# First MLP's in-projection of two of six token blocks in 2x2 block products, seven in place of eight, with the weight units combined on GpSimd

## The chip, the cores and the metric

The kernel runs on one core of a Trainium2 chip. Its time is the device time of one execution in microseconds; below are the median and the limits of three runs. One more execution was profiled, and its trace is what the rows come from.

## The reference

Three parts follow each other. Retention attention over 4 batches, 8 heads, 768 steps, 64 wide; then an MLP on 3072 tokens of 512 with a hidden width of 2048; then a gated MLP with a hidden width of 1536.

```
state = gamma * state + k[:, :, t] (x) v[:, :, t]        # per head, 768 steps
y[:, :, t] = scale * q[:, :, t] @ state
x = y, as 3072 rows of 512
h = maximum(x @ w_in, 0);  x = (h * h) @ w_out           # 512 -> 2048 -> 512
xn = x / sqrt(mean(x * x) + 1e-6) * rms_g
out = (silu(xn @ w_gate) * (xn @ w_val)) @ w_out2        # 512 -> 1536 -> 512
```

The weights arrive as 64-bit floats and are turned into float32 on the chip.

## The kernel before

**Arithmetic.** Every product is made of float32r halves: a number is a high part (a cast on ScalarE) and a low part (a subtraction on VectorE, L97), and a product takes three matmuls, high by high, high by low and low by high (`mm3`, L243 to L246). "A step of 12 matmuls" is 4 pieces of the contraction times three.

**Tokens.** The 3072 tokens are six blocks of 512 (0 to 5). Blocks 0 and 1 pass the first MLP in `block1`, hidden piece f = 0 to 15 by piece: 12 matmuls in, relu and square (`act1`), a split into halves named s, 12 matmuls out. Blocks 2 and 3 pass `in_phase(xs)`, 16 hidden pieces f by two blocks t, so that (f, t) names a step, and then `out_1`. Blocks 4 and 5 do the same with `in_phase(xs2)` and `out_2`. Then the second MLP runs in three pairs of blocks.

**Seven products for eight.** `out_1`, `out_2` and the second MLP already work with 2x2 block products: operand sums, seven products P1 to P7, result sums. Their weight operands ("units", 128x2x512, made by `made_units`, L143) lie in DRAM (`uo`, `uo2`) and come one by one into a ring of seven tiles (`ring`, `next_unit`, `unit_done`, L374 to L384); the load of the unit that comes seven later is issued when the products of a unit are done. The in-projection of the first MLP works with plain pieces: in blocks 0 to 3 the weights w_i lie in SBUF, for blocks 4 and 5 they were stored to DRAM (`wi`) and come through the same ring.

**Attention.** It is spread over the first stages as visits: the state and outputs of one chunk of the sequence. A visit's output leaves PSUM banks pr as the operand xh, xl of a later block (`Operand.put`, L262: a copy on ScalarE, a low part on VectorE). A visit scales the state (st) and two operands (vkt, qnt) in advance, many of these on GpSimd (L737, L748, L825).

**Weights.** `tick` (L221) turns one raw weight of 128x512 into float32: `magnitude` on ScalarE (L203) reads the raw tile, two operations on VectorE (L208, L209) finish it, and then the raw load of three steps later is issued on SP (L197). 32 steps serve the first MLP and 36 the second. Ticks are placed by hand between products. ScalarE, VectorE, GpSimd and SP each work in program order, so what is written between two products also stands there in the queue of its engine.

**Order.** The program is written in one order by hand; `between` and `after` callbacks of a phase put work of other engines between the products. The second in-projection has these:

```
for f in range(NF1):
    w = w_of(f)
    for t in range(2):
        proj(w, xs[t], ph[t])
        between(f, t)
        ...
        after(f, t)
```

Of the kernel before, what the change touches and what calls it, by code (L numbers as in the profile page):

```python
# [42 lines left out]
W2_SOON = 20  # L43
OPEN_AT = 12
PREP_IN = 10
# [12 lines left out]
def retention_then_two_mlps(  # L58
# [13 lines left out]
    wi = [dram.tile([128, 2, 512], F32, name=f"wi{f}") for f in range(NF1)]  # L72
# [30 lines left out]
    def sub(out_, a, b):  # L103
        nc.vector.tensor_tensor(out=out_, in0=a, in1=b, op=ALU.subtract)  # L104

    def plus(out_, a, b):
        nc.vector.tensor_tensor(out=out_, in0=a, in1=b, op=ALU.add)  # L107
# [35 lines left out]
    def made_units(to, q, rows, spare):  # L143
        a11, a21 = (rows[0][:, :, h * HALF:(h + 1) * HALF] for h in range(2))
        a12, a22 = (rows[1][:, :, h * HALF:(h + 1) * HALF] for h in range(2))
# [8 lines left out]
        plus(sm, a21, a22)  # L154
        sub(a21, a11, a21)
# [3 lines left out]
        sub(sm, sm, a11)  # L159
        put(P7, a21)  # L160
        yield
        sub(a12, a12, sm)
# [85 lines left out]
    class Operand:  # L248
# [13 lines left out]
        def put(self, o, banks):  # L262
            n = KC // len(banks)
            for k, src in enumerate(banks):
                a = slice(n * k, n * k + n) if self.whole else slice(0, n)
                h, l = (t[0 if self.whole else k][:, a, o] for t in self.t)
                split(h, l, src, nc.vector)

# [226 lines left out]
    def prep_x(j, y, subs_first=False):  # L495
# [14 lines left out]
        def put(k, src):  # L510
            X[k] = [slot("xop", F32R) for _ in range(2)]
            split(*X[k], src, nc.vector)
# [120 lines left out]
    ORDER = (P2, P1, P5, P6, P7, P3, P4)  # L633

# [45 lines left out]

    with tc.manual_schedule():
# [24 lines left out]
        def load_v(c):  # L706
            nc.sync.dma_start(both[c], vk[c])
# [295 lines left out]

        def early0(f):
            tick(low_first=at[0] < 5, ahead=at[0] > 8)

        def late0(f):
            tick(low_first=at[0] < 5)

# [6 lines left out]
        def factory(q):  # L1016
            rows = [slot("rows") for _ in range(2)]
            for r in range(2):
                for c in range(2):
                    w = W[("o", 4 * q + 2 * r + c)].bitcast(F32)  # L1020
                    plus(rows[r][:, c, :], w[:, 0, :], w[:, 1, :])
                    yield
            yield from made_units(uo, q, rows, lambda: cf.tile([128, 512], F32, tag="f", name="sm"))

        def all_units():
            for q in range(NQ):
                yield from factory(q)

        def keep_out(f):
            keep_units(uo, f, W[("o", f)])  # L1030
            nc.sync.dma_start(wi[f], W[("i", f)].bitcast(F32))

        xs = []
        made = all_units()
# [12 lines left out]

        def last1(f):
            stores()
            if f >= 5:  # L1050
                for _ in range(3):
                    next(made, None)

        block1(1, cur, sink1, (0, 2, 4, 6, 8, 10, 12, 14), early1, keep_out, last1)
# [6 lines left out]
        def sink2(c):  # L1061
            t = c // B - 4
            if t == len(xs2):
                xs2.append(Operand(t == 0))
# [16 lines left out]
        stream += wi  # L1081
# [9 lines left out]
        def after1(f, t):  # L1091
# [11 lines left out]
            elif f % 2 == 0 and f < 8:  # L1103
                tick()
            if t or f not in (2, 4, 6, 8):
                make_some()
            if 2 * f + t >= 24 and len(ring) < 7:
# [9 lines left out]
        while at[0] < upto[0] or at[0] - 1 in done:  # L1117
            tick()
# [5 lines left out]
        while makers:  # L1124
            make_some()
        stores()
        out_1.hi(3)

        def extra1(n, y):
            if n == NOUT - 7:  # L1130
                more_steps(len(steps))
            if NOUT - 4 <= n < NOUT - 2:
                tick()

# [28 lines left out]
        def between2(f, t):  # L1163
            background()
            if (f, t) == (3, 0):
                sums(pa[0])
            if f == OPEN_AT and t == 0:
# [4 lines left out]
            if f >= 8 and next(prep_count) < PREP_IN:  # L1172
                next(prep[0], None)

        prep_count = iter(range(10 ** 6))

        def after2(f, t):
            if t == 1:
                unit_done()
            if f < OPEN_AT and (t == 0 or f in (2, 6)):  # L1180
                stores()
                tick()
            if t == 1 and 3 <= f < 7:
                if f == 3:
                    yn.extend(big(f"yn{t_}") for t_ in range(2))
                h, t_ = ((1, 0), (0, 0), (0, 1), (1, 1))[f - 3]
                nc.sync.dma_start(yn[t_][:, 2 * h:2 * h + 2, :], ys[t_][:, 2 * h:2 * h + 2, :])
            if f == 5 and t == 0:
                prep[0] = prep_x(0, {(h, t_): yn[t_][:, 2 * h:2 * h + 2, :] for h in range(2) for t_ in range(2)}, True)
                next(prep[0])  # L1190
            if (f, t) in ((13, 1), (14, 1)):
                out_2.hi(f - 13)
                out_2.lo(f - 13)
            if f == 15:
                if t:
                    out_2.lo(2)
                out_2.hi(2 + t)

        def w_of2(f):
            return next_unit()  # L1200

        in_phase(xs2, w_of2, after2, between2)
        next(prep[0], None)
# [9 lines left out]
        def extra2(n, y):  # L1213
            if n == 0:
# [192 lines left out]
```

## Time and profile before

| | us |
|---|---|
| median of 3 runs | 1104.43 |
| lowest, highest | 1103.22, 1105.47 |
| span of the profiled execution, first to last instruction | 1102.2 |
| TensorE busy in it | 1093.3 |
| VectorE, ScalarE, GpSimd busy | 732.5, 544.9, 64.3 |

The profiled execution has no time of its own beside its span; the median of the runs is 2.2 us above it. Stages by the trace, in us from the span's start: block 0 from 16 to 115, block 1 to 235, the in-projection of blocks 2 and 3 to 342, `out_1` to 419, the in-projection of blocks 4 and 5 to 506, `out_2` to 584, the second MLP to the end. TensorE's granted clock is 1.00 (2.4 GHz) in all of them.

### The profile page before, as it was taken

The page shows a single profiled execution, that of the slowest core. Times are in us where ns is not written, and L with a number is a line of the kernel's source. Part 1 is how long each engine was busy: PE and PEld are TensorE (multiplying, and loading weights), DVE is VectorE, ACT ScalarE, POOL GpSimd, SP SyncE. Part 2 cuts the span into 40 slices and gives each one's busy share as a digit, 9 for nine tenths or more (in the row PEclk, how much of TensorE's full clock was granted, in tenths as well). Part 3 has the DMA queues.
Part 4 walks back from the last instruction along what each step waited for, and adds up shares of the span by engine and source line. Part 5 has one row for each costly group of instructions (what it writes and reads, how often), then busy time and mean ns, then how long its engine had stood idle before and what let it go on. Part 6 is the DMA issues. An engine that isn't in the chain of part 4 may idle for free.

```text
span 1102.2 us, 16497 instructions
## 1 busy us (share of the span) xinstructions
PE 1093.3 (99%) x6340; PEld 899.8 (82%) x6340; DVE 732.5 (66%) x1040; ACT 544.9 (49%) x854; POOL 64.3 (6%) x58
## 2 busy tenths in 40 slices
PE   8999999999999999999999999999999999999998
PEld 6888888888887888888888888888888888888887
DVE  6988448968866873365877677996333797333585
ACT  4777434447756436566445635553232554333442
POOL 0000132214220000000000000000000000000000
PEclk9999999999999999999999999999999999999999
DMA  9942557898995669964655778767558567555563
GB/s 353 376 164 99 210 210 286 293 385 306 348 334 195 216 238 353 332 216 166 209 195 207 273 265 309 245 212 255 195 212 265 193 211 250 195 195 195 193 212 115
DMA packets 92814, 266.76 MB, mean 242 GB/s; under 512 B 9768, under 2 KB 27072, under 8 KB 92736
## 3 DMA queue, kind: packets, MB, share of 16 engines
q1 hardware_dynamic: 92592, 265.58, 67.6%
q8 instruction: 50, 0.82, 0.3%
q14 instruction: 28, 0.23, 0.1%
q10 hardware_dynamic: 144, 0.13, 0.0%
HBM read 190.69 MB, written 74.99 MB: 241 GB/s over the span
## 4 chain that ended last, share of the span: by engine, by line
PE 97%; DVE 1%; DMA 1%; ACT 1%; SPq 0%; issue 0%
PE ph L276 23%; PE ph L244 9%; PE ph L245 9%; PE ph L246 9%; PE pa L244 7%; PE pa L246 7%; PE pa L245 7%; PE pb L244 4%; PE pb L246 4%; PE pb L245 4%; PE pr L244 3%; PE pr L246 3%; PE pr L245 3%; PE pr L805 2%; PE pr L814 1%; PE pr L794 1%
## 5 line engine op out<-in xcount | busy, mean ns | idle before, releaser
L276 PE MATMUL ph<-xh,w_i 128*128 128x512 f32 x512 | 165.7, 393 | 0.9 <-ACT xh L891 0.8
L437 ACT CAST o<-act 128x1024 fp32r<-128x1024 f32 x101 | 105.6, 1052 | 107.7 <-DVE act L104 46.6
L97 DVE TENSOR_TENSOR o<-act,o 128x1024 fp32r<-128x1024 f32 x101 | 122.9, 1220 | 40.0 <-ACT o L437 40.0
L276 PEld LDWEIGHTS ph<-xh,w_i 128*128 128x128 f32 x512 | 95.9, 188 | 23.3 <-ACT xh L891 1.1
L276 PE MATMUL ph<-xl,w_i 128*128 128x512 f32 x256 | 99.3, 390 | 0.0
L245 PE MATMUL ph<-o,ring 128*128 128x512 f32 x228 | 88.9, 390 | 0.0
L246 PE MATMUL ph<-o,ring 128*128 128x512 f32 x228 | 88.8, 390 | 0.0
L244 PE MATMUL ph<-o,ring 128*128 128x512 f32 x228 | 88.8, 389 | 0.0
L276 PE MATMUL ph<-xh,ring 128*128 128x512 f32 x256 | 79.5, 390 | 0.0
L107 DVE TENSOR_TENSOR part<-pr,part 128x512 f32<-128x512 f32 x36 | 24.6, 690 | 54.4 <-ACT part L111 54.4
L396 ACT ACTIVATE act<-ph 128x512 f32<-128x512 f32 x64 | 38.2, 596 | 43.4 <-PE ph L276 43.4
L630 ACT ACTIVATE t<-part 128x512 f32<-128x512 f32 x54 | 34.1, 632 | 47.0 <-DVE part L107 47.0
L111 ACT COPY part<-ph 128x512 f32<-128x512 f32 x50 | 29.0, 587 | 56.6 <-PE ph L246 56.6
L276 PEld LDWEIGHTS ph<-xh,ring 128*128 128x128 f32 x256 | 48.1, 188 | 10.4 <-ACT act L396 0.2
L244 PE MATMUL ph<-xop,ring 128*128 128x512 f32 x144 | 56.3, 391 | 0.0
L244 PE MATMUL pb<-xop,ring 128*128 128x512 f32 x144 | 56.2, 390 | 0.0
L245 PE MATMUL ph<-xop,ring 128*128 128x512 f32 x144 | 56.1, 390 | 0.0
L246 PE MATMUL pb<-xop,ring 128*128 128x512 f32 x144 | 56.1, 389 | 0.0
L246 PE MATMUL ph<-xop,ring 128*128 128x512 f32 x144 | 56.1, 389 | 0.0
L245 PE MATMUL pa<-xop,ring 128*128 128x512 f32 x144 | 56.1, 389 | 0.0
L245 PE MATMUL pb<-xop,ring 128*128 128x512 f32 x144 | 56.1, 389 | 0.0
L246 PE MATMUL pa<-xop,ring 128*128 128x512 f32 x144 | 56.1, 389 | 0.0
(215 smaller groups left out, 2528.1 us busy)
## 6 DMA issues: line engine op xcount, KB each, us to landing
ring<-wu SPq DMA_DIRECT2D x84, 512.0 KB, 4.3
ring<-up SPq DMA_DIRECT2D x63, 512.0 KB, 4.2
ring<-uo SPq DMA_DIRECT2D x56, 512.0 KB, 3.8
wu<-ring SPq DMA_DIRECT2D x42, 512.0 KB, 5.0
vkt<-vk SPq DMA_DIRECT2D x20, 512.0 KB, 3.9
raw<-w1i SPq DMA_DIRECT2D x16, 512.0 KB, 5.7
raw<-w1o SPq DMA_DIRECT2D x16, 512.0 KB, 8.6
wi<-w_i SPq DMA_DIRECT2D x16, 512.0 KB, 6.4
```

What stands on the lines that cost most here:

```text
L97: eng.tensor_tensor(out=dst_l, in0=src, in1=dst_h.bitcast(F32), op=ALU.subtract)
L107: nc.vector.tensor_tensor(out=out_, in0=a, in1=b, op=ALU.add)
L111: nc.scalar.copy(dst[:, m], acc[m])
L244: nc.tensor.matmul(acc, ah, bh, start=start, stop=False, **more)
L245: nc.tensor.matmul(acc, ah, bl, start=False, stop=False, **more)
L246: nc.tensor.matmul(acc, al, bh, start=False, stop=stop, **more)
L276: nc.tensor.matmul(h, w[:, a, k * 128:(k + 1) * 128], x[b][k], start=n == 0, stop=n == len(order) - 1)
L396: nc.scalar.activation(a, ph[t], AF.Relu)
L437: nc.scalar.copy(h, src)
L630: nc.scalar.activation(t, g, AF.Silu)
L794: nc.tensor.matmul(kv[b, p, :], kk[:, p, h, :], vv[:, p, h, :], start=True, stop=True)
L805: nc.tensor.matmul(a[heads[h ^ SWAP[p]], :], vv[:, p, h, :], P[:, h, p, :], start=(p == 0 or two and p == 2), stop=(c < B and p in (1, 3)) ...
```

## The change

- The in-projection of blocks 4 and 5 becomes `in_pair(n)`, n = 0 to 3. Each n makes 512 of the 2048 hidden values for both blocks, by seven products of 12 matmuls in the order P1, P2, P6, P5, P7, P3, P4: 4 x 7 x 12 = 336 matmuls, where 32 x 12 = 384 stood. P1, P6, P7 and P4 run on in one pair of accumulators (ph or pb by turns), with copies to SBUF (`take`, on ScalarE) after P1 and P6 before the next product is added; P2 stands in pr, P5 and P3 in pa. Results are added on VectorE, relu and square are on ScalarE, mostly 1024 wide.
- The weight operands of these products, `ui`, are made in blocks 1 to 3 by `in_units` and stored to DRAM (28 units; of each seven, those of P1, P2 and P4 are quarters of w_i itself, stored by `keep_in`): 16 sums of high and low parts on GpSimd, 16 sums and differences and 16 low parts on VectorE, 16 casts on ScalarE. The stores of `wi` go. The ring loads 28 units where it loaded 16.
- The units `uo` of `out_1` are made earlier: the first group of four in block 0, f = 9 to 15, wholly combined on GpSimd, the rest in block 1 from f = 2. The sums of high and low parts move to GpSimd for all of them.
- The visits of the third stage only copy their output (`Raw`); sums, differences and halves of it are made by `raw_x` in seven units of `out_1` (X_AT) and after P1 and P2 of n = 0.
- Ticks: 19 in place of 20 steps of the second MLP stand in the stages before `out_1`, and in the third stage only at t = 0; three stand in `out_1` at n < 3, and three at its end; the rest stand after P2, P6, P7 and P4 of n = 0, 1, 2, and a loop after P4 of n = 2 takes what is left. The preparation of the second MLP's operands (`prep_x`) is spread over n = 2 and 3.

```diff
-W2_SOON = 20
+W2_SOON = 19
+X_AT = (11, 12, 17, 18, 23, 24)
...
+    class Raw:
+        def put(self, o, banks):
+            n = KC // len(banks)
+            for k, src in enumerate(banks):
+                nc.scalar.copy(self.t[:, n * k:n * k + n, o], src)
...
+    def in_pair(n, after):
+        a00, a11, a01, a10 = (slot("act") for _ in range(4))
...
+        main = (ph, pb)[n % 2]
+        def both(k, acc, start):
+            u = units(next_unit())
+            for m in range(2):
+                product(acc[m], u, k, m, start)
+            unit_done()
+        both(P1, main, True)
+        take(a00, main)
+        after(n, P1)
+        both(P2, pr, True)
+        add(a00, pr)
+        for a in last_square:
+            relu_square(a)
+        after(n, P2)
+        both(P6, main, False)
+        take(a01, main)
+        relu_square(a00)
+        after(n, P6)
+        both(P5, pa, True)
+        take(a11, pa)
...
+        both(P7, main, False)
+        add(a11, main)
...
+        both(P3, pa, False)
+        add(a01, pa)
+        relu_square(a11)
...
+        both(P4, main, False)
+        for m in range(2):
+            nc.scalar.activation(a10[:, m], main[m], AF.Relu)
+        nc.scalar.activation(a10, a10, AF.Square)
+        last_square[:] = [a01]
+        after(n, P4)
...
+        def factory(q):
...
+                    plus(rows[r][:, c, :], w[:, 0, :], w[:, 1, :], nc.gpsimd)
+                    yield
+            yield from made_units(uo, q, rows, lambda: spare, False, nc.gpsimd if q == 0 else None)
...
         def late0(f):
+            stores()
             tick(low_first=at[0] < 5)
+            if f >= 9:
+                next(made)
+                if f < 11:
+                    next(made)
...
+        def in_units():
             for q in range(NQ):
+                for r in range(2):
+                    for m in range(2):
+                        w = W[("i", 4 * q + 2 * r + m)].bitcast(F32)
+                        plus(rows[r][:, m, :], w[:, 0, :], w[:, 1, :], nc.gpsimd)
+                yield
+                yield from made_units(ui, q, rows, lambda: cf.tile([128, 512], F32, tag="f", name="sm"), True)
...
         def sink2(c):
-                xs2.append(Operand(t == 0))
+                xs2.append(Raw())
...
+        steps2 = {(0, k): 1 for k in (P6, P7, P4)}
+        steps2 |= {(1, k): 1 for k in (P2, P6, P7, P4)} | {(2, k): 1 for k in (P2, P6, P7, P4)}
...
+        def after2(n, k):
             background()
...
+            if (n, k) == (2, P4):
                 while at[0] < upto[0] or at[0] - 1 in done:
                     tick()
                 stores()
                 open_late()
+            elif (n, k) in steps2:
+                tick()
+            if n == 0:
+                next(coming_x, None)
...
-        in_phase(xs2, w_of2, after2, between2)
+        for n in range(NQ):
+            in_pair(n, after2)
+        for a in last_square:
+            relu_square(a)
```

On GpSimd, in the third stage between the visits of steps (3,1) and (5,1), the program of before has these rows (st is the state, y an output of the first MLP, vkt and qnt operands of the next visits):

```order
L825 TENSOR_TENSOR st1_225<-st1_225,sdec_sb_223 128x256
L353 TENSOR_TENSOR y_2646<-y_2646,y_2647 128x512
L748 TENSOR_TENSOR vkt_2773<-vkt_2773,vdec_sb_222 128x512
L737 TENSOR_TENSOR qnt_2934<-qnt_2934,qdec_sb_221 128x512
L825 TENSOR_TENSOR st2_226<-st2_226,sdec_sb_223 128x256
```

After the change the same place has these:

```order
L917 TENSOR_TENSOR st1_237<-st1_237,sdec_sb_235 128x256
L106 TENSOR_TENSOR rows_3007<-w_i12_1149 128x512
L106 TENSOR_TENSOR rows_3007<-w_i13_1272 128x512
L106 TENSOR_TENSOR rows_3008<-w_i14_1326 128x512
L106 TENSOR_TENSOR rows_3008<-w_i15_1379 128x512
L363 TENSOR_TENSOR y_2716<-y_2716,y_2717 128x512
L840 TENSOR_TENSOR vkt_2844<-vkt_2844,vdec_sb_234 128x512
L829 TENSOR_TENSOR qnt_3003<-qnt_3003,qdec_sb_233 128x512
```

The four sums of one group of w_i now stand between the scaling of the state and the sum y.

On ScalarE, in the second in-projection, one conversion stood between the relu and square of the steps before (act is the hidden activation, f the magnitude of a raw weight, xop an operand of the second MLP):

```order
L396 ACTIVATE act00_4627<-ph0_204 128x512
L397 ACTIVATE act00_4627<-act00_4627 128x512
L203 ACTIVATE f_4631<-raw_4574 128x512
L100 CAST xop_4649<-yn0_4440 128x1024
L396 ACTIVATE act01_4653<-ph1_205 128x512
L397 ACTIVATE act01_4653<-act01_4653 128x512
```

After the change its queue reads so from the end of n = 2 into n = 3 (pb are the accumulators of n = 3):

```order
L765 ACTIVATE act_4719<-ph0_216 128x512
L765 ACTIVATE act_4719<-ph1_217 128x512
L766 ACTIVATE act_4719<-act_4719 128x1024
L203 ACTIVATE f_4866<-raw_4787 128x512
L203 ACTIVATE f_4873<-raw_4828 128x512
L203 ACTIVATE f_4878<-raw_4870 128x512
L99 CAST xop_4901<-yn0_4575 128x1024
L110 COPY act_4905<-pb0_214 128x512
L110 COPY act_4905<-pb1_215 128x512
L447 CAST o_4927<-act_4402 128x1024
L726 ACTIVATE act_4718<-act_4718 128x1024
```

Three conversions stand in a row, ahead of the copies of P1's sums, which P6 of n = 3 needs done.

On SP the raw loads of those conversions stand so after the change (ring are the seven unit tiles, wq the converted weights in DRAM):

```order
L386 DMA ring4_3678<-ui34_109 128x1024
L181 DMA wq4_144<-f_4757 128x2x256
L197 DMA raw_4828<-w2g 128x1024
L386 DMA ring5_3760<-ui35_110 128x1024
L386 DMA ring6_3811<-ui36_111 128x1024
L181 DMA wq4_144<-f_4783 128x2x256
L197 DMA raw_4870<-w2v 128x1024
L181 DMA wq5_145<-f_4824 128x2x256
```

The last raw load, raw_4870, stands behind the load of ring6, which is issued when the products of P4 of n = 2 have read that tile.

## Rows read from the trace of the kernel before

**Rows 1.** The page's part 1: busy time, share of the span, instructions.

```profile
PE 1093.3 (99%) x6340; PEld 899.8 (82%) x6340; DVE 732.5 (66%) x1040; ACT 544.9 (49%) x854; POOL 64.3 (6%) x58
```

**Rows 2.** The page's part 4: shares of the chain that ended last.

```profile
PE 97%; DVE 1%; DMA 1%; ACT 1%; SPq 0%; issue 0%
```

**Rows 3.** Waits of TensorE: us in total, times, longest.

```profile
PE ph L805 <- DMA stage<-vn: 1.9, 1, 1.9
```

**Rows 4.** Windows: length, PE, PEld, DVE, ACT, POOL busy, PEclk, DMA share, GB/s.

```profile
16.00:115.00 99.00, 97.89 (x779) 79.35 (x776) 85.68 (x164) 68.57 (x133) 5.11 (x6) 1.00 0.65 238
115.00:235.00 120.00, 120.00 (x1070) 98.84 (x1069) 79.11 (x145) 49.64 (x89) 32.53 (x28) 1.00 0.71 258
235.00:342.00 107.00, 106.55 (x926) 86.99 (x925) 77.92 (x148) 72.62 (x132) 25.46 (x20) 1.00 0.92 334
342.00:419.00 77.00, 76.54 (x337) 63.38 (x338) 57.40 (x56) 33.13 (x38) 0.00 (x0) 1.00 0.64 223
419.00:506.00 87.00, 87.00 (x397) 71.48 (x396) 39.99 (x54) 56.84 (x89) 0.00 (x0) 1.00 0.78 275
...
73.00:115.00 42.00, 42.00 (x335) 34.81 (x334) 34.83 (x68) 27.27 (x53) 1.44 (x2) 1.00 0.42 153
91.00:97.00 6.00, 6.00 (x28) 4.96 (x27) 5.83 (x15) 2.63 (x9) 0.64 (x1) 1.00 0.99 381
```

**Rows 5.** The chain in order of time: start, us, engine, name, line, count.

```profile
438.57 68.40 PE ph L276 x300
```

**Rows 6.** Timeline of TensorE: start, us, engine, line, operation [idle before, releaser].

```profile
82.03 0.39 PE L245 MATMUL pa<-s,w_o 128*128 128x512 f32 x1
...
271.40 0.69 PE L794 MATMUL pr<-vkt 128*64 128x64 f32 x16
...
342.46 0.50 PE L244 MATMUL pr<-oh,ring 128*128 128x512 f32 x1 [0.92 <-DVE xl L97]
```

**Rows 7.** Timeline of GpSimd.

```profile
143.26 1.29 POOL L737 TENSOR_TENSOR qnt<-qnt,qdec_sb 128x512 f32<-128x512 f32 x1
...
200.22 1.73 POOL L737 TENSOR_TENSOR qnt<-qnt,qdec_sb 128x512 f32<-128x512 f32 x1
...
264.05 0.93 POOL L825 TENSOR_TENSOR st<-st,sdec_sb 128x256 f32<-128x256 f32 x1 [6.47 <-DVE st L107]
264.94 1.74 POOL L353 TENSOR_TENSOR y<-y 128x512 f32<-128x512 f32 x1
266.64 1.04 POOL L748 TENSOR_TENSOR vkt<-vkt,vdec_sb 128x512 f32<-128x512 f32 x1
```

**Rows 8.** Timeline of VectorE.

```profile
79.65 0.69 DVE L97 TENSOR_TENSOR s<-r,s 128x512 fp32r<-128x512 f32 x1
...
200.72 1.78 DVE L97 TENSOR_TENSOR made<-sm,made 128x512 fp32r<-128x512 f32 x1
```

**Rows 9.** Timeline of ScalarE.

```profile
417.63 0.59 ACT L111 COPY y<-ph 128x512 f32<-128x512 f32 x1 [3.98 <-PE ph L246]
419.48 1.06 ACT L365 ACTIVATE y<-y 128x1024 f32<-128x1024 f32 x1
...
464.65 0.67 ACT L203 ACTIVATE f<-raw 128x512 f32<-128x512 f32 x1 [2.75 <-DMA raw<-w2g]
468.42 1.03 ACT L100 CAST xop<-yn 128x1024 fp32r<-128x1024 f32 x1
```

**Rows 10.** Timeline of SP's queue.

```profile
450.32 4.34 SPq L498 DMA_DIRECT2D rr<-rrs  x2
...
456.13 0.56 SPq L197 DMA_DIRECT2D raw<-w2g  x1
```

**Rows 11.** DMA issues: count, KB each, median us from issue to landing.

```profile
raw<-w2g SPq DMA_DIRECT2D x12, 512.0 KB, 5.9
raw<-w2v SPq DMA_DIRECT2D x12, 512.0 KB, 8.5
ring<-wi SPq DMA_DIRECT2D x16, 512.0 KB, 6.6
```

More of the change, by code (lines that the diff above doesn't have):

```diff
@@ L493, in retention_then_two_mlps, with raw_x, put, prep_x @@
     mix = None
[L495 removed]
+    def raw_x(raws, to):
+        y = {(h, t): raws[t].t[:, 2 * h:2 * h + 2, :] for h in range(2) for t in range(2)}
+        def put(k, src, wide=False):
+            if wide:
+                t = big("xop", F32R)
+                to[k] = [t[:, 0:2], t[:, 2:4]]
+            else:
+                to[k] = [slot("xop", F32R) for _ in range(2)]
+            split(*to[k], src, nc.vector)
+        put(P2, y[1, 0])
+        yield
+        put(P1, y[0, 0])
+        yield
+        sub(y[0, 0], y[0, 1], y[0, 0], nc.gpsimd)
+        put(P3, y[1, 1])
+        yield
+        sub(y[0, 1], y[1, 1], y[0, 1], nc.gpsimd)
+        put(P5, y[0, 0])
+        yield
+        sub(y[1, 1], y[1, 1], y[0, 0], nc.gpsimd)
+        yield
+        put(P6, y[1, 1])
+        sub(y[1, 0], y[1, 0], y[1, 1], nc.gpsimd)
+        yield
+        put(P7, y[0, 1], True)
+        yield
+        put(P4, y[1, 0], True)
+        yield
+    def prep_x(j, y, to, subs_first=False):
         rr = [tp.tile([128, TB], F32, tag="y", name="rr") for _ in range(2)]
@@ L510, in put @@
         def put(k, src):
-            X[k] = [slot("xop", F32R) for _ in range(2)]
-            split(*X[k], src, nc.vector)
+            to[k] = [slot("xop", F32R) for _ in range(2)]
+            split(*to[k], src, nc.vector)
         yield
@@ L1002, in block1, with all_units, keep_out @@
                 prev = (f, s, j)
+        def factory(q):
+            rows = [slot("rows") for _ in range(2)]
+            for r in range(2):
+                for c in range(2):
+                    w = W[("o", 4 * q + 2 * r + c)].bitcast(F32)
+                    plus(rows[r][:, c, :], w[:, 0, :], w[:, 1, :], nc.gpsimd)
+                    yield
+            spare = slot("sm")[:, 0, :] if q == 0 else cf.tile([128, 512], F32, tag="f", name="sm")
+            yield from made_units(uo, q, rows, lambda: spare, False, nc.gpsimd if q == 0 else None)
+        def all_units():
+            for q in range(NQ):
+                yield from factory(q)
+        def keep_out(f):
+            keep_units(uo, f, W[("o", f)])
+        made = all_units()
         def early0(f):
+            stores()
             tick(low_first=at[0] < 5, ahead=at[0] > 8)
         def late0(f):
+            stores()
             tick(low_first=at[0] < 5)
+            if f >= 8:
+                keep_out(f - 8)
+            if f >= 9:
+                next(made)
+                if f < 11:
+                    next(made)
         nxt = Operand(True)
@@ L1080, in retention_then_two_mlps @@
         stream += [uo[q][k] for k, q in out_1.seq]
-        stream += wi
+        stream += [ui[q][k] for q in range(NQ) for k in IN_ORDER]
         stream += [uo[q][k] for k, q in out_1.seq]
```

155 lines of the change are left out of this document (86 added, 69 removed).

## The prediction

> **What bounds the kernel now.** I read the page's busy times first: TensorE is at work for 1093.3 of 1102.2 us, VectorE for 66%, ScalarE for 49%, GpSimd for 6% [rows 1]. The chain of work that ended last says the same in another way, 97% of it is TensorE [rows 2]. Waits of TensorE are few; the longest is one of 1.9 us at the start [rows 3]. So the only thing that shortens this kernel is less work for TensorE, and any wait that the change puts into TensorE's stream counts in full. Then the windows by stage, for the room that the other engines have: VectorE is free for 13.3, 40.9, 29.1, 19.6 and 47.0 us in block 0, block 1, the in-projection of blocks 2 and 3, its out-projection and the second in-projection (stage less busy time, 99.00-85.68 and so on), and the transfers are near full in the third stage, at a share of 0.92 [rows 4]. The span ends 2.2 us below the median of the three runs (1104.43); I sum against the span and add 2.2 back.
>
> **Matmuls taken away: -10.9.** The second in-projection falls from 32x12 = 384 to 4x7x12 = 336 matmuls of 128x512. On the chain a stretch of 300 such matmuls takes 68.40 us, 0.228 each [rows 5]. 48 x 0.228 = 10.9. That stage's stretch runs without a gap now (87.00 busy of 87.00, [rows 4]), so all of it is on the path.
>
> **The visits' operand: -0.4.** The last visit now ends in a VectorE low part that reads PSUM pr, and TensorE waits 0.92 for it before it writes pr again [rows 6]. After the change ScalarE alone copies, so a part of the wait stays: half a 0.9, -0.4 (bounds 0 and -0.9). The lows that this takes from VectorE come back as 7 lows of 1024 wide, most of them in out_1, in units where VectorE has no subtraction of its own; VectorE is free for 19.6 us there and 7 x twice 0.69 is 9.7, hidden, 0. Without the cover it would show at the first product, whose operands are made first.
>
> **Weight units.** GpSimd gets 36 operations of 512 wide: 32 sums, 16 of them VectorE's until now, and 4 of the first group's. What GpSimd costs VectorE is in the rows of block 1: a 128x512 operation of GpSimd alone takes 1.04 or 1.29, beside a busy VectorE 1.73 [rows 7]; the VectorE operation that falls beside it takes 1.78 in place of 0.69 [rows 8], so 0.7 to 1.1 lost. In block 1 and the in-projection stand 28 of them, 28 x 1.1 = 31, and VectorE's own work grows by 8 operations (32 for the new units, less 16 sums and 8 of the first group), 8 x 0.69 = 6: 37 against 70 us free. Hidden on the average, 0; the places that matter are narrow ones:
>
> Block 0, f=9 to 15: VectorE gets 8 GpSimd operations beside it (8 x 0.73 to 8 x 1.1 = 5.8 to 8.8) and 4 new lows (2.8), 8.6 to 11.6 together. It is free for 7.2 us of the 42 from 73 to 115 [rows 4], and its low part of s, done at 80.34, is used at 82.03 [rows 6, 8], a lead of 1.7 to 1.9. That covers 9.1. The middle of the two ends, 10.1, is late by 1.0: **+1.0** (0 to 2.5).
>
> The visit in the in-projection's step (5,1): GpSimd scales st at 264.05, adds y at 264.94 and makes vkt at 266.64, done at 267.68 [rows 7]; TensorE takes vkt at 271.40 [rows 6], a slack of 3.7. Now four sums stand between st and y (GpSimd's rows of the order), 4 x 1.29 to 4 x 1.73 = 5.2 to 6.9. Their inputs have long been there, but GpSimd waits for st's input until 264. If all four come after it, TensorE waits 1.5 to 3.2; some VectorE idleness and the y that can go at once spare part: 0 to 2.5, taken **+0.9**. TensorE would be seen waiting for vkt.
>
> Here a rule of the Trainium skill speaks against the change ("SBUF — State Buffer", section "Who interferes with whom"): VectorE and GpSimd share a port pair under an exclusive lock, and a VectorE operation with two SBUF inputs that is issued second stays blocked until GpSimd's has finished. The rows of 200.22 and 200.72 bear it out for one pair: VectorE's ends 0.55 us behind GpSimd's. By the rule every sum could cost VectorE its whole 1.29 or more, in place of my 0.7 to 1.1; that is a rival, priced below from rows.
>
> **The last raw weights: +6.6.** This is the largest cost. Four ticks that stood one by one now stand in one heap after P4 of n=2 (ScalarE's rows of the order: three magnitudes in a row, then the cast of xop, then the copy of pb to act that frees P1's sums for P6 of n=3). The last raw load stands on SP's queue behind a load of a ring tile that waits for P4's last matmul, and behind a store, so it is issued about 1 us after P4's end (each SP issue takes about half a microsecond, [rows 10]). From issue to landing such loads take 5.9 and 8.5 (medians, [rows 11]); I take the mean, 7.2. ScalarE's wait for such a load is seen now already, 2.75 us of it at 464.65 [rows 9]. Then 0.67 for the magnitude, 1.03 for the cast and 0.59 for the first copy [rows 9]: 1 + 7.2 + 0.67 + 1.03 + 0.59 = 10.5 after P4's end. TensorE has P1 and P2 meanwhile, 24 x 0.227 = 5.4. So P6 starts 5.1 late. A second wait follows, since from that copy to the first copy of pa after P5 ScalarE has queued three casts of 1.03, four squares and relus of 1024 wide at 1.06 and four copies of 0.59 [rows 9], 9.7 against three products, 8.2: 1.5. Together 6.6, with ends 0 (the load lands within 2 us, or is issued earlier) and 7.9 (8.5 in place of 7.2).
>
> **Transfers.** 28 unit loads take the place of 16 in the second in-projection, 14.7 MB against 8.4, and as much more, 6.3 MB, is stored in blocks 1 to 3. Now the second in-projection moves 275 GB/s at a share of 0.78 [rows 4]; its 23.9 MB and 6.3 more in 76 us are 398 GB/s, or some 370 without the three ticks that move to out_1 with their half a megabyte in and out; 381 at 0.99 is what a full stretch moves [rows 4]. That is close to full, so landings at the upper end are likely. But a ring of seven tiles gives a load 6 x 2.72 = 16 us from issue to need, and they land in 6.6 [rows 11]: 0, unless the landing more than doubles. SP is also held 4.34 us at 450.32 by a pair of loads that wait for their source [rows 10]; these come as before, 0.
>
> **Sum**: -10.9 - 0.4 + 1.0 + 0.9 + 6.6 = -2.8 of 1102.2, so a span of 1099.4 and a time of **1101.6**. What a measurement of this kernel can tell from no change is about 0.2%, 2.2 us: 1102.2 to 1106.6.
>
> **Rivals.**
> *The heap is hidden.* If the last load lands in 2 us or is issued earlier, ScalarE is back before P6; what is left is -10.9 - 0.4 and stalls of 0 to 3: 1093 to 1096.5, say 1095. For: SP could be idle at that place, and the medians are of loads that share the queue with others. Against: the 2.75 at 464.65. Chance 0.30.
> *The transfers saturate.* Landings grow in the second in-projection. With the heap's load at 10 in place of 7.2 its term is 9.4, and I give 0.5 to a wait in the in-projection of blocks 2 and 3, at a share of 0.92 now: 1104.9. For: raw weights already take 8.5 at half of the places. The larger stores fall partly into the third stage. Against: three raw loads leave the second in-projection. Chance 0.14.
> *Slower: GpSimd's sums hold VectorE for their whole length.* Place: block 0, and f=5 and f=11 of block 1, where four sums stand in a row. At 1.29 to 1.73 a sum, block 0 has 10.3 to 13.8 + 2.8 against 9.1, 4.0 to 7.5 late, where 1.0 is counted; each of the two bursts has 5.2 to 6.9 in an f with 2.6 us free (40.9/16) and the lead of 1.9, so 0.7 to 2.4. That puts 4.4 to 11.3 more, 1106.0 to 1112.9, middle 1109. It decides from where a sum costs VectorE more than 1.1. For: the pair at 200.72. Against: in the same rows GpSimd is stretched from 1.04 and 1.29 to 1.73, so VectorE gets in between. Chance 0.13.
>
> **How the numbers follow.** My forecast (1099 to 1104) has 0.43; a little over half of it and the whole first rival lie below 1102.2, with a trace of the saturated case: faster 0.57. The rest of the forecast and two thirds of the saturated case: same 0.26. Slower 0.17. The range runs from 1093.0 (no stall at all) to 1106.0 (the heap at its upper end with both narrow places at theirs); only the third rival and a little more lie outside.
>
> **What would show it.** Right: the second in-projection has 336 matmuls at 0.228; one wait of TensorE of about 5 us on ScalarE's copy of pb, with ScalarE waiting for a raw load before it; a second of 1 to 2 us four products on; vkt late once near 271. Wrong: no such wait on pb (first rival), waits on raw or ring tiles in many places (second), or waits on s or w_o lows in block 0 from f=9 with the 128x512 operations of VectorE at 1.5 to 2 us (third). The likeliest error of mine is the landing time of one transfer.

## The result: slower by 0.9%, and the profile after

The changed kernel takes 1114.76 us (median of 4 runs, 1112.97 to 1116.24), the kernel before beside it 1104.53: a ratio of 1.0092, 95% interval [1.0076, 1.0107]. The forecast was 1101.6, faster or the same, with a range up to 1106.0: wrong in sign and outside the range. The profiled execution took 1113.58, its span is 1111.8, 9.6 more than before.

The page's part 1 of the changed kernel, and the shares of its chain (answers to [rows 1, 2]):

```profile
PE 1088.1 (98%) x6292; PEld 890.5 (80%) x6292; DVE 789.8 (71%) x1067; ACT 567.3 (51%) x873; POOL 132.4 (12%) x98
...
PE 82%; DVE 7%; DMA 6%; ACT 3%; issue 2%; SPq 1%; ACTq 0%; DVEq 0%
```

The 48 matmuls are gone (6340 to 6292). At 0.228 each TensorE's busy time should have fallen to 1082.4; it is 1088.1. Some matmuls ran at a lower clock (below), and short waits count as busy, since a matmul is shown as 0.39 us long where the next can start after 0.228. Also, 15% of the chain has left TensorE. The longest of its waits are these (us in total, times, longest); before, 0.9 and 0.3 were all behind the first 20 us:

```profile
PE pb L244 <- ACT act L110: 5.4, 1, 5.4
PE pr L245 <- DVE o L96: 3.4, 2, 2.5
PE ph L286 <- DVE causal L874: 1.6, 2, 1.1
...
PE ph L286 <- DVE w_i L96: 1.2, 1, 1.2
PE ph L286 <- ACT act L406: 0.9, 1, 0.9
PE ph L244 <- issue: 0.8, 1, 0.8
...
PE ph L244 <- DVE act L106: 0.7, 1, 0.7
...
PE pa L245 <- DVE ol L96: 0.7, 1, 0.7
PE pb L244 <- DVE act L106: 0.6, 1, 0.6
```

I marked the same matmul in both timelines of TensorE at each stage's edge. Differences of these marks say where the 9.6 us are:

| stretch | before, us | after, us | difference | forecast |
|---|---|---|---|---|
| to the second visit of block 0 | 62.13 | 61.84 | -0.3 | 0 |
| from there to block 1's first visit | 58.85 | 63.00 | +4.15 | +1.0 |
| to the first product of `out_1` | 221.48 | 222.84 | +1.4 | +0.5 |
| `out_1` | 76.34 | 78.32 | +2.0 | 0 |
| second in-projection | 88.01 | 86.54 | -1.5 | -4.3 |
| `out_2` | 76.16 | 80.23 | +4.1 | 0 |
| the second MLP to the end | 519.2 | 519.0 | -0.2 | 0 |

**Block 0.** VectorE's and then GpSimd's timeline from 68.8 us, the first sums of the new program:

```profile
68.81 0.42 DVE L208 TENSOR_SCALAR f<-f 128x512 int32<-128x512 int32 x1
...
70.17 1.78 DVE L96 TENSOR_TENSOR w_i<-f,w_i 128x512 fp32r<-128x512 f32 x1
71.87 1.52 DVE L208 TENSOR_SCALAR f<-f 128x512 int32<-128x512 int32 x1
73.42 0.69 DVE L209 SCALAR_TENSOR_TENSOR f<-raw,f 128x512 int32<-128x512 int32 x1
```

```profile
69.66 3.44 POOL L106 TENSOR_TENSOR rows<-w_o 128x512 f32<-128x512 f32 x2
74.24 3.32 POOL L106 TENSOR_TENSOR rows<-w_o 128x512 f32<-128x512 f32 x2 [1.14 <-ACT f L203]
```

Beside GpSimd's sums a low part lasts 1.78 in place of 0.69, a shift 1.52 in place of 0.42: 1.09 and 1.10 more for the two sums of 69.66, so a sum costs VectorE 1.1 us. From 67 to 114 us VectorE has hardly a gap left, and TensorE then waits for it (timeline of TensorE):

```profile
106.98 0.73 PE L286 MATMUL ph<-xh,w_i 128*128 128x512 f32 x2 [1.22 <-DVE w_i L96]
...
116.44 0.50 PE L286 MATMUL ph<-xh,w_i 128*128 128x512 f32 x1 [1.13 <-DVE causal L874]
```

**out_1.** The same with raw_x's four subtractions of 1024 wide (raw_x stands after six units of `out_1`, not seven); GpSimd and VectorE:

```profile
384.05 6.66 POOL L103 TENSOR_TENSOR raw<-raw 128x1024 f32<-128x1024 f32 x2 [53.81 <-DVE xop L96]
```

```profile
385.02 3.42 DVE L103 TENSOR_TENSOR act<-act,act 128x1024 f32<-128x1024 f32 x1
388.37 3.42 DVE L96 TENSOR_TENSOR ol<-act,oh 128x1024 fp32r<-128x1024 f32 x1
391.71 1.21 DVE L103 TENSOR_TENSOR act<-act,act 128x1024 f32<-128x1024 f32 x1
```

Each takes 2.2 us from VectorE, which would do it itself in 1.22. TensorE's waits here are the two of 0.7 (on ol) and 0.8 (issue) in the list above.

**The second in-projection.** Windows (columns as in [rows 4]):

```profile
426.00:490.00 64.00, 63.32 (x291) 51.34 (x290) 36.87 (x58) 47.16 (x65) 0.00 (x0) 1.00 1.03 400
490.00:495.00 5.00, 0.81 (x4) 0.34 (x2) 1.37 (x3) 1.20 (x3) 0.00 (x0) 0.78 0.83 309
495.00:500.00 5.00, 3.81 (x10) 3.05 (x11) 4.93 (x7) 4.92 (x7) 0.00 (x0) 0.54 0.48 119
```

For 64 us the transfers are at 400 GB/s and a share of 1.03, full. Then TensorE stands still, and its granted clock falls: a mean of 0.54 in the last window is the lower level, 1.2 GHz, for most of it. SP's queue, ScalarE and TensorE around it:

```profile
486.29 0.42 SPq L197 DMA_DIRECT2D raw<-w2v  x1
```

```profile
494.06 0.66 ACT L203 ACTIVATE f<-raw 128x512 f32<-128x512 f32 x1 [3.80 <-DMA raw<-w2v]
494.62 1.03 ACT L99 CAST xop<-yn 128x1024 fp32r<-128x1024 f32 x1
495.56 1.07 ACT L110 COPY act<-pb 128x512 f32<-128x512 f32 x2
```

```profile
496.19 0.79 PE L244 MATMUL pb<-xop,ring 128*128 128x512 f32 x1 [5.38 <-ACT act L110]
496.78 0.63 PE L245 MATMUL pb<-xop,ring 128*128 128x512 f32 x1
```

This is the chain that was forecast, row by row: P1 of n=3 starts at 485.21, which is P4's end; the load is issued 1.1 us later, ScalarE has it 7.8 us later, and TensorE waits 5.38 (forecast 5.1). The eight matmuls behind it take 3.5 us in place of 1.8, most of them 0.43 us apart in place of 0.228: 1.7 us that I had not counted. The second wait of the forecast, on ScalarE's copy of pa, did not come. Instead TensorE waits twice for sums of VectorE (act L106), 0.7 before P4 of n=2 and 0.6 before P4 of n=3, which I had not counted either.

**The start of out_2.** TensorE, VectorE and ScalarE:

```profile
520.89 0.50 PE L245 MATMUL pr<-o,ring 128*128 128x512 f32 x1 [2.53 <-DVE o L96]
```

```profile
518.48 1.23 DVE L96 TENSOR_TENSOR xop<-yn,xop 128x1024 fp32r<-128x1024 f32 x1 [2.45 <-ACT xop L99]
519.62 1.22 DVE L96 TENSOR_TENSOR o<-act,o 128x1024 fp32r<-128x1024 f32 x1
```

```profile
517.41 1.03 ACT L99 CAST xop<-yn 128x1024 fp32r<-128x1024 f32 x1
518.35 1.04 ACT L447 CAST o<-act 128x1024 fp32r<-128x1024 f32 x1
```

The operand o of the third product is late because a cast and a low of xop, an operand for the second MLP that is not due before 592, stand in front of it on both engines. The fourth product waits another 0.9, again for a low of o that stands behind one of xop. With the slow restart after each, these two waits are 4.0 of the 4.1 us.

### The profile page after: what moved, and what is told of

The parts are those of the page before. It is cut to its first block, busy times and chain, and to the rows that moved or that the text cites. A ratio compares the mean times of both kernels' runs of the same rounds, so it can differ in the third digit from the quotient of the medians.

```text
span 1111.8 us, 16597 instructions
## 1 busy us (share of the span) xinstructions
PE 1088.1 (98%) x6292; PEld 890.5 (80%) x6292; DVE 789.8 (71%) x1067; ACT 567.3 (51%) x873; POOL 132.4 (12%) x98
## 4 chain that ended last, share of the span: by engine, by line
PE 82%; DVE 7%; DMA 6%; ACT 3%; issue 2%; SPq 1%; ACTq 0%; DVEq 0%
PE ph L286 12%; PE ph L244 8%; PE ph L245 8%; PE ph L246 8%; PE pa L244 7%; PE pa L245 7%; PE pa L246 7%; PE pb L246 4%; PE pb L244 4%; PE pb L245 4%; PE pr L245 3%; PE pr L244 3%; PE pr L246 3%; PE pr L897 1%; DMA raw<-w1i 1%
## 5 line engine op out<-in xcount | busy, mean ns | idle before, releaser
L244 PE MATMUL pb<-xop,ring 128*128 128x512 f32 x176 | 69.5, 395 | 6.0 <-ACT act L110 5.4
L244 PE MATMUL ph<-xop,ring 128*128 128x512 f32 x176 | 68.8, 391 | 0.7 <-DVE act L106 0.7
L245 PE MATMUL pb<-xop,ring 128*128 128x512 f32 x176 | 69.1, 393 | 0.0
L246 PE MATMUL pb<-xop,ring 128*128 128x512 f32 x176 | 69.0, 392 | 0.0
L244 PE MATMUL pa<-xop,ring 128*128 128x512 f32 x176 | 68.6, 390 | 0.0
L246 PE MATMUL ph<-xop,ring 128*128 128x512 f32 x176 | 68.5, 389 | 0.0
L245 PE MATMUL ph<-xop,ring 128*128 128x512 f32 x176 | 68.5, 389 | 0.0
L245 PE MATMUL pa<-xop,ring 128*128 128x512 f32 x176 | 68.5, 389 | 0.0
L246 PE MATMUL pa<-xop,ring 128*128 128x512 f32 x176 | 68.5, 389 | 0.0
L103 DVE TENSOR_TENSOR act<-act 128x1024 f32<-128x1024 f32 x52 | 63.4, 1219 | 0.3
L106 DVE TENSOR_TENSOR part<-pr,part 128x512 f32<-128x512 f32 x36 | 24.6, 690 | 54.5 <-ACT part L110 54.4
L286 PEld LDWEIGHTS ph<-xl,w_i 128*128 128x128 f32 x256 | 48.1, 188 | 9.6
```

Of the source, the lines that this page charges most:

```text
L103: eng.tensor_tensor(out=out_, in0=a, in1=b, op=ALU.subtract)
L106: eng.tensor_tensor(out=out_, in0=a, in1=b, op=ALU.add)
L244: nc.tensor.matmul(acc, ah, bh, start=start, stop=False, **more)
L245: nc.tensor.matmul(acc, ah, bl, start=False, stop=False, **more)
L246: nc.tensor.matmul(acc, al, bh, start=False, stop=stop, **more)
L286: nc.tensor.matmul(h, w[:, a, k * 128:(k + 1) * 128], x[b][k], start=n == 0, stop=n == len(order) - 1)
```

## The experiments

Each has its median and its ratio to the kernel before, measured beside it; the changed kernel is at 1114.76. Executions of one kernel lie 1 to 7 us apart, and the second visit of block 0 alone comes at 61.8 to 64.6 us in the profiled ones, so differences of 1 to 2 us are read from the marks.

**Eight sums alone in the kernel before.** (`eng` is GpSimd in the first run, VectorE in the second.)

```diff
 def late0(f):
     tick(low_first=at[0] < 5)
+    if f in (9, 10, 12, 14):
...
+        for i in range(2):
+            w = W[("o", ...)].bitcast(F32)
+            eng.tensor_tensor(out=extra_sum[0][:, i, :], in0=w[:, 0, :], in1=w[:, 1, :], op=ALU.add)
```

> The kernel before with nothing but eight sums of 128x512 on GpSimd added in block 0 (two after each of f=9, 10, 12 and 14; their result is not used). Theory: each keeps VectorE out for about 1.08 us; pairs cost 2.2 us of VectorE, most of which its gaps and lead can't take, so block 0 grows by 2 to 4 us: 1106.5 to 1108.5. Rival: it was the four lows, casts and stores of the first group that delayed block 0, GpSimd beside VectorE costs nothing on the path: 1104 to 1105.

> The same eight sums on VectorE instead, at the same places: 8 x 0.69 = 5.5 us against 7.2 us free there. Theory: a pair is 1.4 us, within the gap of 0.8 to 1.4 an f and the lead of 1.8: block 0 grows by 0 to 1 us, 1104.3 to 1105.5, less than with GpSimd. Rival: what counts is that anything is added to an engine with so few gaps: as much as on GpSimd.

On GpSimd: 1106.07, 1.0015 [1.0006, 1.0024]. On VectorE: 1104.65, 1.0004 [0.9995, 1.0013], no change that can be told. By the marks block 0 (58.85 us before) takes 61.47 with the sums on GpSimd and 59.74 with them on VectorE, 2.6 and 0.9 more. TensorE's longest wait with GpSimd is a new one:

```profile
PE pa L245 <- DVE s L97: 2.0, 2, 1.0
```

So GpSimd beside a busy VectorE costs more on the path than the same sums on VectorE: the theory. In block 0 the size is within its 2 to 4; the median grew by less, 1.6. The other 1.5 of block 0's 4.15 must come from the rest of what was moved there (lows, casts, stores), which no run takes apart.

**Weight sums on VectorE in the changed kernel** (the argument `nc.gpsimd` dropped in `factory`, `in_units` and for the first group).

> The changed kernel with all 36 sums and differences of the weight units on VectorE, none on GpSimd. Theory: each such GpSimd operation keeps VectorE out for 1.08 us, and VectorE itself does it in 0.69; block 0 gets 8 x 0.39 = 3.1 us back and the stall of 0.7 in block 1 goes, TensorE's delay at the end of block 0 falls from 4.2 to about 1: 3 to 5 us less, 1110 to 1112. Rival: the loss of block 0 comes from the four new lows and casts and the earlier stores, and VectorE is full anyway: within 1 us of 1114.8, or more.

1112.08, 1.0070 [1.0056, 1.0083]: 2.7 less. From block 0's second visit to block 1's first it now takes 61.29 us, against 63.00 and 58.85 before. The direction is the theory's, the size just under it. In block 0 the move gives 1.7 back, as much as between the two runs above (61.47 to 59.74); of the 2.4 that stay, 0.9 are the sums on VectorE by the run above.

**raw_x's subtractions on VectorE.**

> The changed kernel with the four subtractions of 1024 wide in raw_x on VectorE instead of GpSimd. Theory: they make VectorE operations beside them last 3.3 us and more in out_1, where TensorE loses 2.0 us: that goes, 1112.8 or 1.5 to 2.5 us less than the changed kernel. Rival: VectorE gets 4 x 1.22 = 4.9 us more work there and the loss of out_1 stays or grows: 1114 to 1117.

1113.68, 1.0082 [1.0067, 1.0097]. `out_1` falls from 78.32 to 76.3 us, what it took before, by the marks: 2.0 there, as the theory has it. The medians differ by 1.1 only, which their intervals don't tell from nothing.

**No ui units made.**

> The changed kernel without making and storing the ui units; the second in-projection's products read the uo units instead, so its weights are not w_in's and the output of blocks 4 and 5 is not the reference's. The work on the uo units in block 0 stays. Theory: making ui costs little outside one stall in block 1 (0.7) and one in the in-projection (0.9): 1 to 2 us less, 1113. Rival: the making of ui also holds the transfers and GpSimd in the third stage: 4 us less or more, below 1111.

1113.02, 1.0079 [1.0065, 1.0092]: 1.7 less, as expected (2.2 by the marks, between block 1's first visit and `out_1`). Making the units costs little; the loss is elsewhere.

**Ticks spread over n=0 and n=1.**

```diff
+steps2 |= {(n_, k): 1 for n_ in (0, 1) for k in (P5, P3)}
```

> The changed kernel with four ticks more, after P5 and P3 of n=0 and n=1, so that no heap of ticks is left after P4 of n=2. Theory: the heap's raw load costs 5.4 us of waiting for the copy of pb, about 1.8 us of half clock behind it, and through ScalarE's backlog most of the 3.4 us that TensorE waits for operands of out_2: 8 to 10 us less than the changed kernel's 1114.8, so 1105 to 1107. Rival: the transfers of n=0 and n=1 are full and four more raw loads only move the wait there: less than 4 us gained, above 1111.

1114.63, 1.0094 [1.0077, 1.0111]: nothing gained, the rival is right. The heap is gone, and the wait stands one n earlier, behind ScalarE's wait for raw loads (ScalarE, TensorE):

```profile
474.98 0.66 ACT L203 ACTIVATE f<-raw 128x512 f32<-128x512 f32 x1 [1.74 <-DMA raw<-w2v]
```

```profile
476.16 0.79 PE L244 MATMUL ph<-xop,ring 128*128 128x512 f32 x1 [4.86 <-ACT act L110]
```

My theory that order made this wait fell here. From 440 us up to it the transfers are at a share of 1.04 and 408 to 411 GB/s, which points at bandwidth.

**Half of each unit load.**

```diff
-nc.sync.dma_start(ring[i % 7].bitcast(F32), stream[i])
+nc.sync.dma_start(ring[i % 7].bitcast(F32)[:, :1], stream[i][:, :1])   # for the ui units
```

> The changed kernel in which each load of a ui unit in the second in-projection brings only its first half (256 KB for 512), 7.3 MB less; the other half of the tile is what lay there, so the output of blocks 4 and 5 is not the reference's. Theory: the transfers are full from the start of the in-projection up to the heap (405 GB/s, share 1.03), the raw loads arrive late for that reason, and the wait of 5.4 us for the copy of pb, with the half clock behind it, is the arrears of bandwidth: all of it goes, 1106.5 to 1108, and the waits in out_2 (3.4) stay. Rival: the wait comes from the order alone, the last raw load standing on SP behind a ring load that waits for P4, 1 us plus a landing of at least 5 us even on free queues: a wait of 3 us or more stays, above 1110.

1109.91, 1.0050 [1.0036, 1.0064]: 4.9 less, between the theory's range and the rival's. The transfers fall to a share of 0.91 (window from 426 to 490) and the clock stays up; of the wait this is left:

```profile
PE pb L244 <- ACT act L110: 1.6, 1, 1.6
PE pa L244 <- ACT act L110: 1.4, 1, 1.4
```

The last raw load on SP, and ScalarE behind it:

```profile
485.06 0.42 SPq L197 DMA_DIRECT2D raw<-w2v  x1
```

```profile
490.39 0.66 ACT L203 ACTIVATE f<-raw 128x512 f32<-128x512 f32 x1 [2.04 <-DMA raw<-w2v]
```

ScalarE has the load 5.3 us after its issue, where it took 7.8. But the edit also loosens the order. A load of a whole ring tile leaves 0.2 us after the end of the product that reads the tile; a load of its first half leaves 1.2 us before that end, so that the raw load is issued 0.3 us before P4's end and not 1.1 after it. Of the 3.8 us that the first wait lost, some 2.4 are thus faster transfers and 1.4 the order. So the larger part of the heap's loss, with the half clock, is arrears of bandwidth, as the theory has it, and 3.0 us stay that order makes, as the rival has it. The wait of 1.4 on pa is the second one of my forecast, which the changed kernel doesn't have.

**prep_x's steps earlier.**

```diff
-prep2 = {(2, k): 1 for k in (P1, P2, P5, P3, P4)}
-prep2 |= {(3, k): 1 for k in (P1, P2, P6, P5, P7, P3, P4)}
+prep2 = {(2, k): 1 for k in (P1, P2, P6, P5, P7, P3, P4)}
+prep2 |= {(3, k): 1 for k in (P1, P2, P6, P5, P7)}
```

> The changed kernel with the steps of prep_x moved earlier: after all seven products of n=2 and after five of n=3, so none after P3 and P4 of n=3. Theory: the 3.4 us that TensorE waits for lows of o at the start of out_2 come from casts and lows of xop that stand on ScalarE and VectorE between the last activations and the first operands of out_2; without two of these 2 to 3 us go, 1112 to 1113. Rival: ScalarE's chain from P4's accumulators over relu, square and cast to the low is what is late (4 us from P4's end), whatever stands between: less than 1 us gained.

1112.56, 1.0074 [1.0061, 1.0088]: 2.2 less, and TensorE's wait for o falls from 3.4 to 0.9; `out_2` takes 77.35 us in place of 80.23. The theory holds. In the in-projection waits only change place (on the copy of pb 5.4 to 3.9, on copies of pa from none to 2.6), and it takes 0.4 more.

**The first group in block 1.**

```diff
 def late0(f):
-    if f >= 9: ...
 def last1(f):
-    if f >= 2:
-        for _ in range(2):
-            next(made, None)
+    for _ in range(2):
+        next(made, None)
```

> The changed kernel with the first group of uo units made in block 1 instead of block 0 (two pieces per f from f=0 on), its combinations still on GpSimd. Theory: block 0 has no spare VectorE time, so 8 GpSimd operations at 1.08 each and four lows delay it by 4.2 us; without them the first matmul of block 1 comes when it does in the kernel before, and block 1, where VectorE is free for 41 us, hides them: 1110.5 to 1111.5, 3.3 to 4.3 less than 1114.8. Rival: the GpSimd operations are late wherever they stand, and block 1 now loses what block 0 gains: within 1 us of 1114.8.

1121.52, 1.0148 [1.0127, 1.0168]. Theory and rival both miss. Block 0 is as before (58.86), and block 1 with the stage behind it loses 9.0 by the marks: the pieces end only at the end of block 1, and ScalarE's relu of the next stage stands behind them (2.7 us); a wait of 2.0 on VectorE stands in block 1, and behind both come matmuls at half clock. A bad mend; the work needs a place, not just another block.

**All mends, group one in block 1, with three ticks moved there** (MORE_AT 12, W2_SOON 22), then **the pieces done by f=11** (`range(2 if f < 4 else 3)`), with and without the ticks.

> All mends together: group one in block 1, every combination on VectorE, raw_x's subtractions on VectorE, prep_x's steps earlier as in the run on them, and three ticks moved into block 1 (f=13 to 15) where the transfers have room, so that one tick is left in the heap. Theory: block 0 (4.2), block 1 (0.7), out_1 (2.0), most of the heap (5.4 + 1.8) and of out_2 (3.4) come back: 1098 to 1101, faster than the kernel before by 3 to 6 us. Rival: the arrears of bandwidth stay, since three raw loads are 5 us of the transfers at 405 GB/s and the stage is short of more: 1103 to 1106, no faster than before.

> The run with all mends, and the uo units' pieces done sooner in block 1 (two per f up to f=3, then three, done by f=11), so that no heap of pieces stands at its end and the three ticks at f=13 to 15 have room. Theory: the 5.1 us between the last visit of block 1 and the first of the next stage go: 1101 to 1103. Rival: the engines' work in block 1 is too much wherever it stands: 1106 to 1108 as before.

> The same without the three ticks in block 1 (19 steps before out_1 and the heap of four, as in the changed kernel). Theory: block 1 loses nothing, but the second in-projection pays its arrears of bandwidth: 5 us more than with the ticks moved, 1105 to 1107. Rival: the ticks cost as much in block 1 as they give back later: within 1.5 us of the run with them.

1107.60, 1.0027 [1.0016, 1.0038]; 1109.54, 1.0039 [1.0026, 1.0053]; 1109.89, 1.0043 [1.0031, 1.0056]. All miss their theories; the last one's rival, within 1.5 us, is right. By the marks of the last two the three ticks cost 5.1 us in block 1 and the in-projection after it, and give 4.5 back later: block 1 has no free place either.

**The mends without moved ticks, then four and six ticks into out_1.** The base has the sums and raw_x on VectorE and prep_x earlier, the first group in block 0. The ticks stand after units 21 to 27, or 19 to 27.

> The changed kernel with every combination on VectorE (first group still in block 0), raw_x's subtractions on VectorE and prep_x's steps earlier. Theory: the mends add up, 2.7 + 1.1 + 2.2 less than 1114.8: 1108 to 1109.5, and the heap's waits are what is left above the kernel before. Rival: the mends overlap, since a wait removed at one place is found again at the next: 1110 to 1112.

> The same with four ticks moved from the heap's side into out_1 (after its units 21 to 27 in place of 25 to 27). Theory: 4 raw loads of half a megabyte and their stores are some 7 us of the transfers at 405 GB/s, which out_1 has free; the wait of 4 to 5 us for the copy of pb goes, VectorE in out_1 has 7.5 us free for 4 x 1.1: 4 to 5 us less than without, 1104 to 1105. Rival: VectorE's order in out_1 has no gap where the ticks stand, operands of its products come late there: within 2 us of the run without.

> The same with six ticks moved into out_1 (units 19 to 27). Theory: 6 x 1.1 us take VectorE's 7.5 us there nearly whole, the second in-projection has no arrears left: 1 to 2 us better than with four, 1103 to 1104. Rival: out_1 becomes VectorE's: 1 us or more worse than with four.

1109.06, 1.0036 [1.0021, 1.0051]; 1112.05, 1.0064 [1.0051, 1.0077]; 1109.70, 1.0045 [1.0033, 1.0057]. In the medians the mends add up (2.7 + 1.1 + 2.2 = 6.0, measured 5.7). By the marks they overlap, as the rival has it: the stages up to `out_1` (from block 0's second visit), `out_1` itself and `out_2` give 7.8 back, and the in-projection takes 3.2 more, 89.77. Four ticks make the median 3 us worse and six no better; the theories miss, and so do the rivals. (The base's executions lie from 1106.9 to 1113.7. In the profiled ones `out_1` grows by 4.6 and 7.0 with four and six ticks, and the in-projection shrinks by 5.7 and 8.6, which makes both a little faster.) With six ticks the wait for pb is gone, but one stands ahead of the in-projection, again on raw loads, now 2.7 us apart; the last six reach ScalarE 7 to 9 us after their issue, beside transfers that are full by then (a share of 1.01 to 1.05 from 405 to 430 us):

```profile
PE ph L244 <- ACT y L110: 6.9, 1, 6.9
```

**The same nine ticks after every other unit of out_1**, to unit 26 and to unit 24.

```diff
-if n == NOUT - 8:
+if n == 5:
     more_steps(len(steps))
-if n >= NOUT - 3:
+if n in (8, 10, 12, 14, 16, 18, 20, 22, 24):
+    stores()
     tick()
```

> The mends, and nine ticks in out_1 after its units 10, 12, and so on to 26, the loads of the first issued after unit 7. Theory: the wait of 6.9 us at the start of the in-projection came from raw loads 2.7 us apart that take over 7 to land; 5.4 us apart they are there, that wait and the half clock behind it go, and the heap stays away: 1101 to 1103, faster than the kernel before. Rival: VectorE has 7.5 us free in out_1, nine ticks in place of three take 6.6 of them in gaps that are no gaps where they stand, and TensorE waits for lows of o as long as it waited for y: 1106 to 1109.

> The same with the nine ticks after units 8, 10, and so on to 24, the first loads after unit 5. Theory: the last ticks are clear of out_1's last additions, and the in-projection finds ScalarE idle: as the run to unit 26 or up to 1 us better, 1100 to 1103. Rival: earlier ticks fall on raw_x's pieces (units 11, 12, 17, 18) and make TensorE wait in out_1: 1106 to 1109.

1100.49, 0.9959 [0.9946, 0.9971], and 1098.21, 0.9942 [0.9929, 0.9956]: faster than both kernels, and a little faster than the theories had it. `out_1` still takes its 76 to 77 us. In the window from 424 to 490 of the second one TensorE has no gap. The transfers move less over this window than in the changed kernel, though up to 474 us they are at a share of 0.98 to 1.03:

```profile
424.00:490.00 66.00, 66.00 (x305) 54.27 (x304) 43.72 (x62) 51.40 (x68) 0.00 (x0) 1.00 0.96 345
```

From P2 of n=0 (in the kernel before: as far into its stage) to the second MLP it takes 153.15 us against 161.45: 8.3 of the 10.9 are there, and TensorE's waits there are 1.8. In the in-projection alone it is 78.56 against 88.01, 9.5 less. Block 0 keeps its loss, 61.30 against 58.85.

**The ticks alone**, without the other mends.

> The changed kernel with nothing but nine ticks in out_1 after its units 8, 10, and so on to 24. Theory: the heap, its half clock and the waits around it are the largest single loss; without them 6 to 9 us less than 1114.8, 1106 to 1109, and block 0, raw_x and prep_x keep the rest above the best run. Rival: with raw_x's subtractions on GpSimd out_1 has no VectorE time for six more ticks, so that the wait moves into out_1: above 1110.

1110.02, 1.0054 [1.0040, 1.0068]: 4.7 less, at the edge of the rival's range. The heap is gone, but as the rival has it, with raw_x on GpSimd `out_1` has a new wait (TensorE's waits):

```profile
PE pa L245 <- DVE ol L96: 3.8, 1, 3.8
```

On top of the other mends the same order of ticks is worth 10 to 11 (1109.06 to 1098.21 in the medians; the in-projection goes from 89.77 to 78.56). It needs the VectorE time that GpSimd took.

## Why the prediction was wrong

- **Matmuls taken away, -10.9: right.** 48 fewer; in the best run 9.5 of it is seen in its stage, and 8.3 up to the second MLP.
- **The visits' operand: -0.4 measured -0.46** (the wait of 0.92 is 0.46), but "hidden, 0" for raw_x was a step that failed. I priced its lows and left out its four subtractions on GpSimd, each 2.2 us of VectorE: +2.0 in `out_1`, gone with these on VectorE.
- **Weight units in block 0, +1.0: 4.15.** The price of a sum, 0.7 to 1.1, is 1.1 every time; with it my own sum is 8.8 + 2.8 - 9.1 = 2.5. What failed besides is that gaps and lead were counted as one store of 9.1 us: eight sums alone, 8.8 on GpSimd or 5.5 on VectorE, already made block 0 2.6 and 0.9 longer. Sums come in pairs of 2.2 us, and a gap later on doesn't pay for them; that this is the reason is argued, not shown. The third rival named this place with chance 0.13; block 0's part of it, 4.0 to 7.5, holds the 4.15, but its bursts in block 1 cost 0.7 together, not 1.4 to 4.8. VectorE loses 1.1 by a sum, about what such an operation takes GpSimd alone (1.04 in [rows 7]), not the stretched 1.73 up to which I priced it. GpSimd's stretch is no sign that VectorE gets in between, as I took it: 1.73 is about 1.04 and the 0.69 of one VectorE operation, as if the two took turns by whole operations. By the rule of the Trainium skill ("SBUF — State Buffer", "Who interferes with whom") whoever issues second is blocked for the other's whole operation. The rows agree with that: 1.78 for a low of 0.69 is 1.09 more.
- **The visit at (5,1), +0.9: none.** vkt was there in time, 1.0 us before its use; the visit itself had become 4.4 us later. 0.9 was lost in the same stage at 288 us, on ScalarE's relu (L406).
- **The last raw weights, +6.6: right in order, nearly in size, and the size partly by luck.** The first wait is 5.4 against 5.1. The second, 1.5, did not come; two waits of 0.7 and 0.6 on VectorE's sums, and 1.7 of half clock, stand in its place and were not in the sum. The landing of 7.2 was taken from medians of 5.9 and 8.5; the load took 7.8 beside full transfers and 5.3 beside less full ones, so the middle of those medians happened to hold what the full transfers do.
- **Transfers, 0: the mechanism that failed in the in-projection.** I had worked out 370 to 398 GB/s against 381 and still put it at nothing since the ring has 16 us of slack. The ring had; the raw loads had not. I put the heap's wait down to order alone. The run with half loads (2.4 of the 3.8 us that went, and the half clock) and spreading the ticks, which only moved the wait, show arrears of bandwidth for the larger part of it.
- **out_2 was left out of the sum: +4.1, the largest step that failed.** I followed the change to the end of the loop that it rewrites and not to the first operands behind it. Of its waits for o the one of 2.5 went with prep_x's steps moved; the one of 0.9 stayed, and with its restart it is the 1.2 that `out_2` still takes more.

The forecast's -2.8 and the measured +9.6 differ by 12.4: block 0 3.2, the stages to `out_1` 0.9, `out_1` 2.0, the in-projection 2.8, out_2 4.1, less 0.5 of the ends.

## What to carry to other kernels

Work moved to an idle GpSimd is not free for a busy VectorE: here a sum of 512 takes 1.1 us of VectorE's time on GpSimd and 0.69 on VectorE itself, so it pays only where VectorE is idle. When fewer matmuls are bought with more bytes, ask whether the stage's transfers are full afterwards, and which loads have the least slack; spreading these within the full stage moves the wait, and only a stage with free transfers pays it, with the loads spaced there too. Spare time counts where it stands: put a stage's free time against each burst, not against the sum, and follow a rewritten loop to the first operands of the stage behind it.

## What the runs showed of the hardware that was not expected

- The cost of a GpSimd operation was the same for two kinds of VectorE operation: 1.10 more for a shift of 0.42, 1.09 for a low of 0.69; 2.2 for operations of 1024 on both.
- After a wait of 5.4 us TensorE's granted clock is at 1.2 GHz for eight matmuls, most of them 0.43 us apart; it falls while TensorE waits. The length of the wait alone doesn't tell the price: with the ticks spread, twelve matmuls ran so after a wait of 4.9 us, and with the pieces done by f=11, nine after one of 1.9. The clock stayed at 1.00 at the wait of 2.5 us in `out_2`, and in the half-load run, whose longest waits between 490 and 512 us are 1.6 and 1.4.
- The transfers reach 400 GB/s at a share of 1.03 over 64 us, and at most 412 in its windows of 10 us. Loads of 512 KB take 7.5 us for the ui units in that stretch, and 3.5 for the uo units elsewhere (medians); in the kernel before, at 275 GB/s, the loads of wi in that stretch took 6.6 and those of uo 3.8, so the full transfers themselves add less than this difference.
